# Centred x for the first two V and z2 blocks: an attention and gMLP kernel on one Trainium2 core

## The chip, the core and the metric

The kernel runs on one core of one Trainium2 chip. The core has TensorE (matrix products, written PE in the profile), VectorE (DVE), ScalarE (ACT), GpSimd (POOL), and SyncE (SP), which here only issues DMAs. Every engine works through its own instruction queue in order, and engines wait for one another by semaphores. Results of TensorE go to PSUM, which is used here as 8 banks of 128 x 512 fp32. Everything else lies in SBUF, 128 partitions wide. The metric is the device time of one execution in microseconds.

## The reference

For x of shape 2048 x 512 the reference adds a windowed attention and a gated MLP to x. Both start from the same normalised x.

```python
xn = layernorm(x)                                  # over 512, no gain or bias
qkv = xn @ wqkv                                    # 32 heads of 16; wqkv is 512 x 1536
logits[s, w] = q[s] . k[s - 2w] / 4                # w = 0..7; positions before 0 masked
o = softmax(logits over w) @ v[s - 2w]
a = o @ wo

z = gelu(xn @ w_in)                                # w_in is 512 x 1792
z1, z2 = z[:, :896], layernorm(z[:, 896:])
g = w_sp @ z2 + b_sp                               # w_sp is 2048 x 2048
out = x + a + (z1 * g) @ w_out                     # w_out is 896 x 512
```

V and z2 both have the form f(xn @ W). A row of xn is (x - mean) * rstd, so a row of xn @ W is rstd times a row of (x - mean) @ W. All matrices are bf16; sums are fp32.

## The kernel before

The 2048 rows of x are 16 blocks of 128 rows (b = 0 to 15), in four groups j of 512 rows. Nothing is written in program order by hand. The code adds tasks to a `Plan`, each with an engine, a function, an estimated duration, the buffers it reads and writes, and a priority (a low number goes first). `schedule` (line 121) then simulates the five engines with these estimates and puts the tasks of each engine in an order. At each step it takes, on the engine that can start earliest, the task with the lowest priority number among those ready within 40 ns of the first. It also picks the PSUM bank (`place`, line 148). `emit` (line 254) writes each engine's instructions in that order with the waits they need. On the chip the order is fixed: a task behind a late one waits too.

The stages around the change:

- **Loads** (lines 497 to 536). Block 0 of x is loaded in two halves of 64 partitions, one issued by SP and one by ACT (line 521). ACT then issues x1 and x2 (line 499). SP issues the halves of the V weights (wv, line 503), the halves of the z2 weights (w_in2, line 509), the other blocks of x, and the weights for Q and K (line 515).
- **Warm-up matmuls** (lines 538 to 543). 22 matmuls on zeros, 10 of 512 columns and 12 of 128, each with a bank of its own and priority 1000, so that the planner uses them where TensorE would otherwise idle.
- **Layer norm** (`ln_block`, line 551). Per block, VectorE computes statistics (L555), their aggregate (L557) and variance + eps (L559, called vpe). POOL raises that to the power -0.5, which is rstd (L561). VectorE then computes xn = (x - mean) * rstd (L563).
- **Transposes.** Blocks 0 to 3 of xn are transposed by TensorE against an identity (L573, four matmuls of 128 x 128) and copied from PSUM to the transposed tile xnT by ScalarE (L579), block 0 in two halves. Blocks 4 to 15 go through a transposing DMA issued by SP (L585).
- **V** (`v_block`, L598). Two tasks of two matmuls per block. ScalarE copies the result (L603) and POOL's queue writes it to a scratch tensor in DRAM (L606), from which shifted windows are read later.
- **z2** (`z2_block`, L696). Eight matmuls of 448 columns per block, then gelu with a row sum (L702) and a square with a row sum (L707) on ScalarE.
- **Q and K** (L615, copied by L624), which need all four blocks of their group. VectorE multiplies and adds the shifted products (L636, L641). z2 is normalised in waves of four blocks (L713 to L726), with POOL's pow at L723.
- **z1** (L740, L746), from the other half of w_in, the tile w_in1 (L771).
- **The tail.** The large product g = w_sp @ z2 (L823) with its copies and products (L831 to L837), the windowed sum over V (L851 to L857), its transposing DMA (L860), and the output products (L879, L888) with the final addition (L894) and store (L899).

The tiles share one arena. The place of w_in1 is used again for two small tiles late in the kernel (line 362).

Of the kernel before, what the change touches and what calls it, by code (L numbers as in the profile page):

```python
# [31 lines left out]
class Task:  # L32
    __slots__ = ("eng", "fn", "est", "name", "dma", "deps", "odeps", "idx", "start", "end", "eng_end", "count",
                 "tok", "clock", "prio", "tbl", "banks", "nwait", "ready", "outs", "used", "late")


class Plan:
# [37 lines left out]
    def add(self, eng, fn, reads=(), writes=(), est=100.0, name="", dma=None, prio=0.0, tbl=None, late=0.0, after=()):  # L75
        t = Task()
        t.eng, t.fn, t.est, t.name, t.dma, t.tbl = eng, fn, float(est), name, dma, tbl
# [43 lines left out]
    def schedule(self, dma_bw=300.0, xbar_bw=190.0, dma_lat=1300.0, dma_pre=400.0, issue=None, tol=40.0):  # L121
# [10 lines left out]
        free["sp"] = 810.0  # L132
# [15 lines left out]
        def place(b):  # L148
# [5 lines left out]
            for o in opts:  # L154
# [7 lines left out]
                key = (mate, av)  # L162
# [4 lines left out]
        while left:  # L167
            pick = None
            for e in ENGS:
                sc = []  # L170
                for t in cand[e]:
                    r = max(t.ready, free[e])
                    for b in t.banks:
                        if b.base is None:
                            p = place(b)
                            if p is None:
                                r = None
                                break
                            r = max(r, p[2])
# [14 lines left out]
            if pick is None:  # L194
                raise RuntimeError("scheduler stuck")
            r, e, t = pick
            for b in t.banks:
                if b.base is None:
                    _, o, av = place(b)
# [11 lines left out]
            if t.dma is not None:  # L211
                iss = issue[e]
# [117 lines left out]
def build_kernel(nc, A_x, A_wqkv, A_wo, B_x, B_w_in, B_w_sp, B_b_sp, B_w_out, out, report=False, emit=True):  # L330
# [12 lines left out]
    NWARM = 22  # L343
# [18 lines left out]
    place(3584, w_in1=0, tg=0, On=2048)  # L362
# [24 lines left out]
    with ExitStack() as es:  # L387
# [41 lines left out]
        for hf in range(2):  # L429
            R1(("xin0", hf), "xin", 256, 256 * hf)  # L430
        for s_ in range(1, NB):
# [25 lines left out]
        for hf in range(2):  # L457
            R(("xnT0", hf), "sb", [(off["xnT"] + dc * S, off["xnT"] + dc * S + 128) for dc in (2 * hf, 2 * hf + 1)])
# [38 lines left out]
        def ld_x(b, eng="sp"):  # L497
            sl = b
            return dma(eng, lambda e: e.dma_start(A("xin", 512, 512 * sl), x2[128 * b:128 * b + 128, :]), 128 * 512 * 2,
                ("xin", sl), writes=[("xin", sl)], name="ldx%d" % b)  # L500
# [19 lines left out]
        for hf, eng in ((0, "sp"), (1, "act")):  # L520
            dma(eng, (lambda hf: lambda e: e.dma_start(ar[64 * hf:64 * hf + 64, off["xin"]:off["xin"] + 512],
                                                       x2[64 * hf:64 * hf + 64, :]))(hf),
                64 * 512 * 2, ("xin0", hf), writes=[("xin0", hf)], name="ldx0_%d" % hf)
# [13 lines left out]

        for wi in range(NWARM):
            bw = plan.bank("warm%d" % wi)
# [427 lines left out]
```

## Time and profile before

| what | value |
|---|---|
| median of 3 runs | 241.43 us (241.14 to 241.65) |
| the profiled execution | 242.69 us |
| its span, first to last instruction | 239.3 us |
| granted TensorE clock, mean | 0.999 |
| busy: TensorE, VectorE, ScalarE, POOL | 234.0, 212.8, 98.1, 33.2 us |
| first V matmul | 7.28 us |
| DMA traffic | 42.81 MB, mean 179 GB/s |

Times in the profile count from the first instruction of the span. A row gives a group of instructions: line, engine, operation, what is written from what, and the shapes. "Idle before" is the time that the engine stood still just before them, and the name behind the arrow is what ended it. PEld is the loading of weights into TensorE, which overlaps with matmuls. Matmuls in a row overlap: one of 512 columns has a duration of 379 ns, but the starts of a row of them lie 216 ns apart. How fast they run is read from the distance of their starts. Some matmul records are missing from the trace (L823 has 440 matmuls to 448 weight loads), which looks like a hole of exactly one matmul.

### The profile page before, as it was taken

To read this page: it belongs to the slowest core of one execution; us is meant where nothing else is said; L and a number is where in the kernel's file an instruction comes from. 1 tells how busy PE (TensorE), PEld (TensorE's weight loads), DVE (VectorE), ACT (ScalarE), POOL (GpSimd) and SP (SyncE) were. 2 spreads that over 40 slices of the span, in tenths; PEclk is the share of its full clock that TensorE was granted. 3 is DMA by queue.
4 is the path that set the end of the run, shared out by engine and by line. 5 is a ranking of instruction groups with operands and counts; after the bars stand their busy time and mean duration, and the time that the engine had idled before them with its cause. 6 is when DMAs were issued, how large, how long until landed. Compare 5 with 4: busy or idle time off the path is not lost.

```text
span 239.3 us, 3165 instructions
## 1 busy us (share of the span) xinstructions
PE 234.0 (98%) x1212; PEld 112.7 (47%) x1233; DVE 212.8 (89%) x267; ACT 98.1 (41%) x144; POOL 33.2 (14%) x56
## 2 busy tenths in 40 slices
PE   7999999999999999999999999999999999999995
PEld 3555555555444444444454444444444444444444
DVE  3798889999989899999999999986898999999952
ACT  2596889899888975541112111001010100101100
POOL 2378350401383500000000000000000000000000
PEclk9999999999999999999999999999999999999999
DMA  5997969993327110004079999999999997942112
GB/s 185 364 316 145 224 151 215 208 208 76 114 108 244 62 37 10 0 8 170 0 228 320 182 245 258 267 168 294 309 344 244 282 325 244 271 141 55 22 44 66
DMA packets 77806, 42.81 MB, mean 179 GB/s; under 512 B 50129, under 2 KB 77153, under 8 KB 77793
## 3 DMA queue, kind: packets, MB, share of 16 engines
q1 hardware_dynamic: 76480, 40.13, 66.2%
q0 software_dynamic: 800, 2.11, 2.8%
q10 hardware_dynamic: 512, 0.38, 0.5%
q8 instruction: 9, 0.15, 0.2%
q14 instruction: 5, 0.03, 0.1%
HBM read 26.35 MB, written 4.21 MB: 128 GB/s over the span
## 4 chain that ended last, share of the span: by engine, by line
PE 69%; DVE 16%; POOL 7%; issue 4%; POOLq 1%; ACT 1%; DVEq 0%
PE ps L823 40%; PE ps L888 10%; PE ps L879 6%; DVE arena L641 5%; PE ps L598 5%; DVE arena L636 4%; PE ps L615 3%; POOL fpool L723 3%; DVE arena L726 2%; PE ps L696 2%; POOL fpool L561 2%; PE ps L541 2%; POOL vscr L606 1%; POOLq L387 1%; DVE arena L563 1%
## 5 line engine op out<-in xcount | busy, mean ns | idle before, releaser
L823 PE MATMUL ps<-arena 128*128 128x512 bf16 x440 | 98.6, 379 | 0.4
L823 PEld LDWEIGHTS ps<-arena 128*128 128x128 bf16 x448 | 43.7, 98 | 52.6
L831 ACT ACTIVATE arena<-ps 128x1024 bf16<-128x1024 f32 (+1 forms) x16 | 14.7, 917 | 104.4 <-PE ps L823 93.8
L636 DVE TENSOR_TENSOR arena<-arena 128x4096 bf16<-128x4096 bf16 x16 | 36.6, 2285 | 0.2
L851 DVE TENSOR_TENSOR arena<-arena 128x4096 bf16<-128x4096 bf16 x16 | 36.5, 2284 | 0.0
L854 DVE TENSOR_TENSOR arena<-arena 128x2048 bf16<-128x2048 bf16 (+1 forms) x32 | 30.5, 953 | 0.4
L615 PE MATMUL ps<-arena 128*128 128x512 bf16 x126 | 28.5, 379 | 0.1
L641 DVE TENSOR_TENSOR arena<-arena 128x4096 bf16<-128x4096 bf16 x12 | 27.5, 2288 | 0.2
L888 PE MATMUL ps<-arena 128*128 128x512 bf16 (+2 forms) x116 | 26.8, 366 | 0.2
L696 PE MATMUL ps<-arena 128*128 128x448 bf16 x128 | 26.0, 352 | 0.0
L740 PE MATMUL ps<-arena 128*128 128x512 bf16 x109 | 24.2, 379 | 0.2
L615 PEld LDWEIGHTS ps<-arena 128*128 128x128 bf16 x128 | 14.5, 113 | 13.0
L894 DVE TENSOR_TENSOR arena<-ps,arena 128x512 bf16<-128x512 f32 (+2 forms) x17 | 11.2, 657 | 9.4 <-PE ps L888 9.4
L624 ACT ACTIVATE arena<-ps 128x1024 bf16<-128x1024 f32 x16 | 16.2, 1019 | 4.3 <-PE ps L615 3.6
L696 PEld LDWEIGHTS ps<-arena 128*128 128x128 bf16 x128 | 12.4, 98 | 11.5
L888 PEld LDWEIGHTS ps<-arena 128*128 128x128 bf16 x119 | 11.6, 98 | 12.7
L740 PEld LDWEIGHTS ps<-arena 128*128 128x128 bf16 x112 | 10.8, 98 | 12.7
L746 ACT ACTIVATE arena<-ps 128x1024 bf16<-128x1024 f32 (+1 forms) x16 | 14.1, 916 | 6.1 <-PE ps L740 6.1
L879 PE MATMUL ps<-arena 128*128 128x512 bf16 (+2 forms) x67 | 16.5, 366 | 0.1
L702 ACT ACTIVATE arena<-ps 128x896 bf16<-128x896 f32 x16 | 14.6, 913 | 2.8 <-PE ps L696 2.6
L598 PE MATMUL ps<-arena 128*128 128x512 bf16 x60 | 14.9, 379 | 0.4 <-ACT arena L579 0.2
L707 ACT ACTIVATE arena<-arena 128x896 bf16<-128x896 bf16 x16 | 15.2, 949 | 0.2
(56 smaller groups left out, 176.4 us busy)
## 6 DMA issues: line engine op xcount, KB each, us to landing
arena<-vscr SPq DMA_DIRECT2D x16, 1024.0 KB, 6.8
arena<-in_A_x_dram SPq DMA_DIRECT2D x29, 128.0 KB, 5.3
vscr<-arena POOLq DMA_DIRECT2D x16, 128.0 KB, 2.8
out_dram<-arena SPq DMA_DIRECT2D x15, 128.0 KB, 5.1
arena<-in_A_wqkv_dram SPq DMA_DIRECT2D x2, 512.0 KB, 6.6
arena<-in_B_w_in_dram SPq DMA_DIRECT2D x2, 448.0 KB, 5.2
arena<-in_B_w_in_dram SPq DMA_DIRECT2D x1, 896.0 KB, 5.3
arena<-in_B_w_out_dram SPq DMA_DIRECT2D x1, 896.0 KB, 5.5
```

Source lines behind the costliest of these rows:

```text
L598: last = t.matmul(P(bk, 512), AC(off["xnT"] + dc * S + 128 * b, [[1, 128]]), AC(off["wv"] + 512 * dc, [[1, 512]]), start=(dc == 0), stop=( ...
L615: last = t.matmul(P(bk, 512, 512 * which), AC(off["wqk"] + 2048 * which + 512 * dc + c, [[4, 128]]), AC(off["xnT"] + dc * S + 512 * j, [[1 ...
L624: T("act", lambda a: a.activation(AC(qo, [[ko - qo, 2], [1, 512]]), P(bk, 1024).rearrange("p (t n) -> p t n", t=2), ACTF.Copy, scale=0.5), ...
L636: T("dve", (lambda pbv, qb, kb: lambda v: v.tensor_tensor(pbv, qb, kb, ALU.mult))(pbv, qb, kb), reads=rd, writes=[("pb", s_)], est=c_tt(40 ...
L641: T("dve", (lambda av, bv: lambda v: v.tensor_tensor(av, av, bv, ALU.add))(av, bv), reads=[("pb", 1)], writes=[("pb", acc)], est=c_tt(4096 ...
L696: last = t.matmul(P(bk, 448, 512 * hf), AC(off["xnT"] + dc * S + 128 * b, [[1, 128]]), AC(off["w_in2"] + 896 * dc + 448 * hf, [[1, 448]]), ...
L740: last = t.matmul(P(bk, 512, 512 * i), AC(off["w_in1"] + 896 * dc + 128 * fc, [[1, 128]]), AC(off["xnT"] + dc * S + 512 * j, [[1, 512]]), ...
L823: last = t.matmul(P(bk, 512, 512 * i), AC(off["z2"] + FH * sh + 128 * fc, [[1, 128]]), AC(off["wT%d" % r_] + sh * 512, [[1, 512]]), start= ...
L851: T("dve", lambda v: v.tensor_tensor(tv, tv, av, ALU.mult), reads=[("attn", b)], writes=[("Vs", sv)], est=c_tt(4096), name="pv%d" % b, pri ...
L854: T("dve", (lambda n: lambda v: v.tensor_tensor(A("Vs", n, 4096 * sv), A("Vs", n, 4096 * sv), A("Vs", n, 4096 * sv + n), ALU.add))(n), wri ...
L879: last = t.matmul(P(bk, cn), AC(off["OT"] + 512 * tb + 128 * cc, [[1, 128]]), AC(off["wo"] + 512 * cc + c0, [[1, cn]]), start=(cc == 0), s ...
L888: last = t.matmul(P(bk, cn), AC(off["z1T"] + fc * S + 128 * tb, [[1, 128]]), AC(off["w_out"] + 512 * fc + c0, [[1, cn]]), start=False, sto ...
```

## The change

For blocks 0 and 1 (`NCEN = 2`) VectorE now computes a centred tile xc = x - mean as soon as the mean is known. TensorE transposes xc, ScalarE copies it in two halves to a new tile xcT, and the V and z2 matmuls of these two blocks read xcT. The factor rstd is applied afterwards, as the per-partition `scale` of the ScalarE instruction that takes V or z2 out of PSUM. The normalised tile of blocks 0 and 1 is still made, transposed by TensorE and copied to xnT, since Q, K and z1 read it; these tasks have priorities behind the centred ones. Blocks 2 and 3 are as before.

Block 0 of x is loaded by one DMA from SP. x1 becomes the first load on ACT's queue. The warm-up is 24 matmuls, 8 of them long, all in one bank, and those left over are dropped once the planner's clock is past 9 us. xc and xcT lie in the place of w_in1, so that w_in1's load, whose code moves behind the V and z2 blocks, must wait for their readers.

The planner's own numbers change too: ordinary loads at 340 GB/s instead of 300, transposing DMAs at 300 instead of 190, 1.45 us of issue time for a transposing DMA instead of 0.48, and banks chosen by when they can be used, with 300 ns against a bank whose neighbour is free, instead of by the neighbour first.

```diff
@@ -118,7 +119,7 @@
...
-    def schedule(self, dma_bw=300.0, xbar_bw=190.0, dma_lat=1300.0, dma_pre=400.0, issue=None, tol=40.0):
+    def schedule(self, dma_bw=340.0, xbar_bw=300.0, dma_lat=1300.0, dma_pre=400.0, issue=None, tol=40.0):
...
@@ -129,7 +130,7 @@
...
         free["pool"] = 500.0
-        free["sp"] = 810.0
+        free["sp"] = 790.0
...
@@ -159,7 +160,7 @@
...
                     mate = 0.0 if (m["prev"] is not None and m["prev"].left > 0) else 1.0
-                key = (mate, av)
+                key = (max(av, now) + 300.0 * mate, av)
...
@@ -192,11 +193,30 @@
...
             r, e, t = pick
+            if t.drop and r > 9000.0:
+                t.start = t.end = t.eng_end = r
+                for b in t.banks:
+                    b.left -= 1
+                    if b.left == 0:
+                        for sl in slots:
+                            if sl["prev"] is b:
+                                sl["avail"] = r
+                cand[e].remove(t)
+                left -= 1
+                for o in t.outs:
+                    o.ready = max(o.ready, r)
+                    o.nwait -= 1
+                    if o.nwait == 0:
+                        cand[o.eng].append(o)
+                continue
...
                 if b.base is None:
-                    _, o, av = place(b)
+                    _, o, av = place(b, max(t.ready, free[e]))
...
@@ -209,7 +229,7 @@
...
             if t.dma is not None:
-                iss = issue[e]
+                iss = 1450.0 if t.dma.get("xbar") else issue[e]
...
@@ -340,7 +360,8 @@
...
     NXT = 4
-    NWARM = 22
+    NCEN = 2
+    NWARM = 24
...
@@ -359,7 +380,7 @@
...
     place(4 * S, xnT=0, OT=0)
-    place(3584, w_in1=0, tg=0, On=2048)
+    place(3584, w_in1=0, tg=0, On=2048, xcT=0, xc=2048)
...
@@ -517,10 +539,7 @@
...
-        for hf, eng in ((0, "sp"), (1, "act")):
-            dma(eng, (lambda hf: lambda e: e.dma_start(ar[64 * hf:64 * hf + 64, off["xin"]:off["xin"] + 512],
-                                                       x2[64 * hf:64 * hf + 64, :]))(hf),
-                64 * 512 * 2, ("xin0", hf), writes=[("xin0", hf)], name="ldx0_%d" % hf)
+        ld_x(0, "sp")
...
@@ -535,12 +554,12 @@
...
+        bw = plan.bank("warm")
         for wi in range(NWARM):
-            bw = plan.bank("warm%d" % wi)
-            n_ = 512 if wi < NWARM - 12 else 128
+            n_ = 512 if wi < 8 else 128
...
                                                        stop=True))(bw, n_),
-              reads=["zeros"], writes=[bw], est=(427.0 if n_ == 512 else 75.0), name="warm%d" % wi, prio=1000)
+              reads=["zeros"], writes=[bw], est=(427.0 if n_ == 512 else 107.0), name="warm%d" % wi, prio=1000, drop=True)
...
@@ -551,41 +570,64 @@
...
             xs_ = b
+            xk = [("xin", xs_)]
             xin = A("xin", 512, 512 * xs_)
-            T("dve", lambda v: v.bn_stats(Fv("st6", 6, 6 * b), xin), reads=([("xin", xs_)] if b else [("xin0", 0), ("xin0", 1)]), writes=[("st6", b)],
+            T("dve", lambda v: v.bn_stats(Fv("st6", 6, 6 * b), xin), reads=xk, writes=[("st6", b)],
...
               writes=[("mv", b)], est=178, name="bnag%d" % b, prio=-1 + b * 0.1)
-            T("dve", lambda v: v.tensor_scalar(Fv("vpe", 1, b), Fv("mv", 1, 2 * b + 1), LN_EPS, None, ALU.add),
-              reads=[("mv", b)], writes=[("vpe", b)], est=140, name="vpe%d" % b, prio=-1.5 + b * 0.1)
-            lnr.append(T("pool", lambda g: g.tensor_tensor(Fv("rstd", 1, b), Fv("vpe", 1, b), Fv("mhalf", 1), ALU.pow),
-                         reads=[("vpe", b), "mhalf"], writes=[("rstd", b)], est=550, name="rstd%d" % b, prio=0))
-            T("dve", lambda v: v.tensor_scalar(A("xn", 512, 512 * sl), xin, Fv("mv", 1, 2 * b),
-                                               Fv("rstd", 1, b), ALU.subtract, ALU.mult),
-              reads=([("xin", xs_)] if b else [("xin0", 0), ("xin0", 1)]) + [("mv", b), ("rstd", b)], writes=[("xn", sl)], est=c_ts(512),
-              name="norm%d" % b, prio=-1 + b * 0.1)
-            if b < NXT:
-                bk = plan.bank("xTr%d" % b)
+            early = b < NCEN
+            xn = A("xn", 512, 512 * sl)
+
+            def pe_tr(src, key, name, prio):
+                bk = plan.bank(name)
...
                     for dc in range(4):
-                        last = t.matmul(P(bk, 128, 128 * dc), A("xn", 128, 512 * sl + 128 * dc), ident, start=True,
+                        last = t.matmul(P(bk, 128, 128 * dc), src[:, 128 * dc:128 * dc + 128], ident, start=True,
...
                     return last
-                T("pe", tr, reads=[("xn", sl), "ident"], writes=[bk], est=4 * c_mm(128), name="xTr%d" % b, prio=0)
-                for hf in ((0, 1) if b == 0 else (None,)):
-                    d0, dn = (0, 4) if hf is None else (2 * hf, 2)
-                    T("act", (lambda d0, dn: lambda a: a.activation(
-                        AC(off["xnT"] + d0 * S + 128 * b, [[S, dn], [1, 128]]),
-                        P(bk, 128 * dn, 128 * d0).rearrange("p (c n) -> p c n", c=dn), ACTF.Copy))(d0, dn),
-                      reads=[bk], writes=([("xnT", b)] if hf is None else [("xnT0", hf)]), est=c_act(128 * dn),
-                      name="xTe%d_%d" % (b, d0), prio=0)
-            else:
-                return dma("sp", lambda e: e.dma_start_transpose(AC(off["xnT"] + 128 * b, [[S, 4], [1, 128]]),
-                                                          A("xn", 512, 512 * sl)),
-                    128 * 512 * 2, ("xT", sl), reads=[("xn", sl)], writes=[("xnT", b)], name="xTd%d" % b,
-                    xbar=True, prio=1)
+                T("pe", tr, reads=[key, "ident"], writes=[bk], est=4 * c_mm(128), name=name, prio=prio)
+                return bk
+
+            if early:
+                xc = A("xc", 512, 512 * b)
+                T("dve", lambda v: v.tensor_scalar(xc, xin, Fv("mv", 1, 2 * b), None, ALU.subtract),
+                  reads=xk + [("mv", b)], writes=[("xc", b)], est=360, name="cen%d" % b, prio=-1 + b * 0.1)
+                bk = pe_tr(xc, ("xc", b), "xTc%d" % b, 0)
+                for hf in range(2):
+                    T("act", (lambda hf: lambda a: a.activation(
+                        A("xcT", 256, 512 * b + 256 * hf), P(bk, 256, 256 * hf), ACTF.Copy))(hf),
+                      reads=[bk], writes=[("xcT", b, hf)], est=c_act(256), name="xTe%d_%d" % (b, hf), prio=0)
+            T("dve", lambda v: v.tensor_scalar(Fv("vpe", 1, b), Fv("mv", 1, 2 * b + 1), LN_EPS, None, ALU.add),
+              reads=[("mv", b)], writes=[("vpe", b)], est=140, name="vpe%d" % b,
+              prio=(-0.5 if early else -1.5) + b * 0.1)
+            lnr.append(T("pool", lambda g: g.tensor_tensor(Fv("rstd", 1, b), Fv("vpe", 1, b), Fv("mhalf", 1), ALU.pow),
+                         reads=[("vpe", b), "mhalf"], writes=[("rstd", b)], est=550, name="rstd%d" % b, prio=0))
+            T("dve", lambda v: v.tensor_scalar(xn, xin, Fv("mv", 1, 2 * b), Fv("rstd", 1, b), ALU.subtract, ALU.mult),
+              reads=xk + [("mv", b), ("rstd", b)], writes=[("xn", sl)], est=c_ts(512),
+              name="norm%d" % b, prio=(0.35 + b * 0.01 if early else -1 + b * 0.1))
+            if b < NXT:
+                bk2 = pe_tr(xn, ("xn", sl), "xTr%d" % b, 0.5)
+                T("act", lambda a: a.activation(AC(off["xnT"] + 128 * b, [[S, 4], [1, 128]]),
+                                                P(bk2, 512).rearrange("p (c n) -> p c n", c=4), ACTF.Copy),
+                  reads=[bk2], writes=[("xnT", b)], est=c_act(512), name="xTn%d" % b, prio=0.5)
+                return None
+            return dma("sp", lambda e: e.dma_start_transpose(AC(off["xnT"] + 128 * b, [[S, 4], [1, 128]]), xn),
+                       128 * 512 * 2, ("xT", sl), reads=[("xn", sl)], writes=[("xnT", b)], name="xTd%d" % b,
+                       xbar=True, prio=1)
+
+        def xTv(b, dc):
+            if b < NCEN:
+                return A("xcT", 128, 512 * b + 128 * dc)
+            return AC(off["xnT"] + dc * S + 128 * b, [[1, 128]])
+
+        def xsc(b):
+            return Fv("rstd", 1, b) if b < NCEN else 1.0
+
+        def xrk(b):
+            return [("rstd", b)] if b < NCEN else []
...
@@ -595,13 +637,13 @@
...
                     for dc in (2 * hf, 2 * hf + 1):
-                        last = t.matmul(P(bk, 512), AC(off["xnT"] + dc * S + 128 * b, [[1, 128]]),
+                        last = t.matmul(P(bk, 512), xTv(b, dc),
...
                     return last
-                T("pe", mm, reads=[("xnT", b) if b else ("xnT0", hf), ("wv", hf)], writes=[bk], est=2 * c_mm(512), name="V%d_%d" % (b, hf),
+                T("pe", mm, reads=[("xcT", b, hf) if b < NCEN else ("xnT", b), ("wv", hf)], writes=[bk], est=2 * c_mm(512), name="V%d_%d" % (b, hf),
...
             T("act", lambda a: a.activation(A("Vn", 512, 512 * sl).rearrange("p (d h) -> p d h", d=16),
-                                            PC(bk.col(), [[1, 16], [16, 32]]), ACTF.Copy), reads=[bk],
+                                            PC(bk.col(), [[1, 16], [16, 32]]), ACTF.Copy, scale=xsc(b)), reads=[bk] + xrk(b),
...
@@ -693,16 +735,16 @@
...
                     for dc in range(4):
-                        last = t.matmul(P(bk, 448, 512 * hf), AC(off["xnT"] + dc * S + 128 * b, [[1, 128]]),
+                        last = t.matmul(P(bk, 448, 512 * hf), xTv(b, dc),
...
                     return last
-                T("pe", mm, reads=[("xnT", b), ("w_in2a", "w_in2b")[hf]], writes=[bk], est=4 * c_mm(448),
+                T("pe", mm, reads=([("xcT", b, 0), ("xcT", b, 1)] if b < NCEN else [("xnT", b)]) + [("w_in2a", "w_in2b")[hf]], writes=[bk], est=4 * c_mm(448),
...
                                             PC(bk.col(), [[512, 2], [1, 448]]),
-                                            ACTF.Gelu_apprx_tanh, accum_out=Fv("s1", 1, b)),
-              reads=[bk], writes=[("z2", b), ("s1", b)], est=c_act(FH, accum=True),
+                                            ACTF.Gelu_apprx_tanh, scale=xsc(b), accum_out=Fv("s1", 1, b)),
+              reads=[bk] + xrk(b), writes=[("z2", b), ("s1", b)], est=c_act(FH, accum=True),
...
@@ -768,13 +810,13 @@
...
-        dma("sp", lambda e: e.dma_start(A("w_in1", 3584).rearrange("p (c n) -> p c n", c=4),
-                                        B_w_in[:, 0:896].rearrange("(c p) n -> p c n", p=128)),
-            512 * 896 * 2, "w_in1", writes=["w_in1"], name="ldwin1", prio=2, after=lnd[4:8])
...
             z2_block(b)
+        dma("sp", lambda e: e.dma_start(A("w_in1", 3584).rearrange("p (c n) -> p c n", c=4),
+                                        B_w_in[:, 0:896].rearrange("(c p) n -> p c n", p=128)),
+            512 * 896 * 2, "w_in1", writes=["w_in1"], name="ldwin1", prio=2, after=lnd[4:8])
```

## The prediction

> **What bounds the kernel now.** I read the page's busy table first, then the stretches (busy time of each engine by stage), then the chain that ended last at both ends, then the opening in order of time.
>
> The page's first table, with the busy time and share of the span:
> ```profile
> span 239.3 us, 3165 instructions
> PE 234.0 (98%) x1212; PEld 112.7 (47%) x1233; DVE 212.8 (89%) x267; ACT 98.1 (41%) x144; POOL 33.2 (14%) x56
> ```
> The stretches; columns after the length are busy time of PE, weight loads, DVE, ACT and POOL with instruction counts:
> ```profile
> 0.00:7.28 7.28, 5.81 (x23) 2.74 (x24) 3.33 (x10) 1.93 (x4) 1.87 (x9) 1.00 0.67 215
> 7.28:14.66 7.38, 7.33 (x43) 3.75 (x45) 5.67 (x20) 5.61 (x11) 3.46 (x6) 1.00 1.09 361
> 14.66:21.57 6.91, 6.91 (x33) 3.61 (x32) 5.99 (x20) 5.39 (x8) 5.49 (x18) 1.00 0.92 190
> 21.57:53.00 31.43, 31.32 (x183) 16.77 (x185) 28.58 (x47) 27.12 (x47) 9.71 (x10) 1.00 1.01 202
> ```
> From 7.28 us, the first V matmul, TensorE idles 0.05, 0.00 and 0.11 us per stretch. So the end is the start of that matmul, plus TensorE's work in a row, plus a tail of 2.8 us (236.5 to 239.3). A gain can come from an earlier start or less TensorE work; an added wait is paid in full. What sets 7.28 is in the opening (start, duration, engine, line, operation, and in brackets the idle time before and its releaser):
> ```profile
> 1.25 5.09 PE L541 MATMUL ps<-arena 128*128 128x512 bf16 x16 [1.25 <-DVE arena L494]
> 3.32 0.69 DVE L555 BATCH_NORM_STATS2 fpool<-arena 128x6 f32<-128x512 bf16 x1 [2.13 <-DMA arena<-in_A_x_dram]
> 4.05 0.18 DVE L557 BATCH_NORM_AGGREGATE fpool<-fpool 128x2 f32<-128x6 f32 x1
> 4.27 0.15 DVE L559 TENSOR_SCALAR fpool<-fpool 128x1 f32<-128x1 f32 x1
> 4.51 0.56 POOL L561 TENSOR_TENSOR fpool<-fpool 128x1 f32<-128x1 f32 x1 [2.93 <-DVE fpool L559]
> 5.13 0.69 DVE L555 BATCH_NORM_STATS2 fpool<-arena 128x6 f32<-128x512 bf16 x1 [0.71 <-DMA arena<-in_A_x_dram]
> 5.75 0.40 DVE L563 TENSOR_SCALAR arena<-arena,fpool 128x512 bf16<-128x512 bf16 x1
> 6.20 0.61 PE L573 MATMUL ps<-arena 128*128 128x128 bf16 x4
> 6.60 0.47 PE L541 MATMUL ps<-arena 128*128 128x128 bf16 x3
> 6.84 0.66 ACT L579 ACTIVATE arena<-ps 128x256 bf16<-128x256 f32 x2 [2.55 <-PE ps L573]
> 7.28 1.04 PE L598 MATMUL ps<-arena 128*128 128x512 bf16 x4 [0.22 <-ACT arena L579]
> 8.15 0.39 PE L573 MATMUL ps<-arena 128*128 128x128 bf16 x4
> ```
> rstd of block 0 is ready at 5.07, but its normalisation runs at 5.75: on VectorE it stands behind block 1's statistics, which wait 0.71 us for x1. The chain of waits over this window is warm-up matmuls, L573, L579, L598. The L541 matmuls start 0.43 us apart for 512 columns; the V matmuls start 0.216 apart ((1.04 - 0.39) / 3). The four transposes take 0.61 us at 6.20 and 0.39 at 8.15. So TensorE runs at half rate up to 6.81 (last start of the three L541) and at full rate by 7.28; the trace's clock record opens at 6.87.
>
> **The change, part by part.** The profiled execution took 242.69 us: its span of 239.3 and 3.4 around it. It stands 1.26 over the median of 241.43. I sum against its span and carry the difference to the median.
>
> *Start of V.* Out of block 0's chain go vpe (0.15), POOL's pow (0.56) with its hops, and the wait behind block 1; in comes a subtraction of 128x512 bf16 (L563's row, 0.40). If x0 lands as before, statistics start at 3.32, the aggregate ends at 4.23, the centring at about 4.67, and TensorE could transpose at 4.72. It is not free: warm-ups stand ahead of it in its in-order queue. Worked from the planner's estimates (read for the order alone: x0 at 3.57, statistics 0.685, aggregate 0.178, centring 0.36), the plan has the transposes ready at 4.90, after 8 long and 4 short warm-ups. On the chip those take 1.25 + 8 x 0.43 + 4 x 0.107 = 5.08 (the first start gap is a little shorter). From the first transpose to the first V took 7.28 - 6.20 = 1.08, which stays: V at about 6.18. Gain 1.09. Bounds: two warm-ups fewer or four more give 5.95 to 6.6, so 1.3 to 0.7.
>
> *x0 whole on SP, x1 first on ACT's queue.* The halves took 0.59 and 0.57 to issue and 2.1 and 2.4 to land. x1's issue moves from 1.42 to about 0.81; beside wv0 on SP it took 0.85 to issue and landed at 5.11, 3.7 later. x0 on one queue lands between 3.0 (as a half) and 4.5 (like x1). Nearest is the half, issued first on an idle queue: 3.0 to 3.6, all hidden under the warm-ups, which cover up to 3.6. Beyond that each us costs one. ACT's queue loses an issue; SP's second issue may slip 0.3, but wv0 (landed 4.73) has 1.4 to spare.
>
> *Half-rate V.* V now starts inside the slow time. From 6.18 to 6.87 is 0.69 us at half rate: 0.34 lost. Bounds 0 (full rate from 6.18) to 0.55 (slow until 7.28).
>
> *Extra transposes.* Blocks 0 and 1 are transposed twice: 8 more matmuls at (0.39 - 0.22) / 3 = 0.056, so +0.44, all on TensorE and all paid.
>
> *Warm-ups behind V0.* 24 instead of 22, 8 of them long. By the same working some three fall among V0, block 1's transposes and V1. 3 x 0.056 = +0.17; bounds 0 to 0.4 (six, some at half rate).
>
> *V1's wait.* Block 1's transposes are queued after V0's first pair, at about 7.04 in slow time; 0.44 to the copy and 0.44 to the matmul (as 6.84 and 7.28 show) against V0's second pair: +0.14; bounds 0 to 0.5. The gap of 0.14 ahead of V at 9.49, where V1 and V2 follow a transpose, goes: -0.14 (bounds 0 to -0.22 with the one at 11.3).
>
> *VectorE and POOL.* Two centrings, +0.8 us of VectorE, lie in its waits before 10 us (0.71 for x1, 0.66 and 0.66 for POOL). Without that cover block 2's normalisation (8.46) slips by as much, and TensorE has z2 of blocks 0 and 1 meanwhile. POOL keeps its two pows; the copies of V0 and z2 of block 0 now wait for rstd, done at 5.07, before them by over 2 us. The normalised blocks 0 and 1 come later, first needed by Q and K at 14.66.
>
> *ScalarE.* Block 1's copy (0.59) becomes two (0.66 together as for block 0), and two whole copies come in (0.59 each): +1.25 us. Idle in 7.28 to 14.66: 7.38 - 5.61 = 1.77, which hides it, and 1.09 more from the earlier start. Four evictions take their scale from a tensor instead of a constant; no row shows that, between 0 and 0.2 us each, off the path, taken as 0. [...]
>
> *w_in1's load* now must wait for the matmuls that read the centred tiles lying in its place (z2 of block 1, about 14 us); it was issued at 20.37 and L740 first reads it at 75.7: nothing.
>
> *The planner.* A transpose DMA is now booked at 1.45 us of issue instead of 0.48 (rows: 28 transposes of activations at 1.2 to 1.6, of w_sp at 2.2), loads are booked faster, banks are chosen by earliest start. The whole order can move. With TensorE idle almost nowhere there is nothing to win; 0 to +1 us, taken as 0, since no wait after 10 us is for a DMA and the last transposed block lands 1.8 us before its matmul (232.35 against 234.13).
>
> Sum: -1.09 + 0.34 + 0.44 + 0.17 + 0.14 - 0.14 = **-0.14 us**: span 239.16, execution 242.55, median **241.3**.
>
> **The rivals.**
> *A, clock early and a clean order.* If full rate comes before 6.18 (-0.34) and neither warm-ups nor a copy stand in V1's way (-0.31), the gain is 0.79: 240.65. For it: nothing ties 6.87 to V. Against: warm-ups begin at 1.25 as before and one profile shows one moment. [...]
>
> *B, ScalarE becomes the bound (slower).* From 21.57 to 53 it is busy 27.12 of 31.43. If the 1.25 us of added copies are not absorbed by 14.66, evictions run late, PSUM banks come free late and TensorE waits for a bank in the Q, K and z2 stage. It decides once more than about 0.6 us is left over; at most 1.25: 241.9 to 242.55. For it: 86% busy there. Against: ScalarE's waits on PE, 0.3 to 0.7 us before Q, K and z2 copies, are slack.
>
> *C, x0 late.* Landing at 3.9 to 4.3 puts V at 6.5 to 6.9: 241.6 to 242.0.
>
> *D, the new order stalls TensorE later.* Some 0.5 to 1 us: 241.8 to 242.3.
>
> **How the numbers follow.** Forecast 0.40, A 0.20, B 0.18, C 0.10, D 0.12. What a measurement here can tell from no change is about 0.2%, 0.48 us: faster is under 240.95, slower over 241.91. Faster: A whole and 0.10 of the forecast, from the fast-clock end alone: 0.30. Slower: 0.16 of B, 0.04 of C, 0.09 of D: 0.29. Within: 0.41. The range 240.6 to 242.3 leaves out 0.07 of A, 0.08 of B and 0.03 of D.
>
> **What would show it.** Right: the first centred transposes at about 5.1, directly behind a warm-up; V at 6.2, its first matmuls 0.43 apart; TensorE idle under 0.3 us from V to 14; L823 starting as densely as before. Wrong: V0 behind a DMA wait of VectorE; TensorE gaps between 14 and 53 with PSUM copies late; full rate seen before 6.2; or TensorE waiting for a transfer after 100 us.

## The result and the profile after

The median after is 250.34 us (249.41 to 251.24, 6 runs) against 241.45 us before in the same comparison (6 runs): a ratio of 1.0359, 95% interval 1.032 to 1.0398. The kernel became 3.6% slower. The prediction said 241.3 us in a range of 240.6 to 242.3, so it is wrong by 9 us. The profiled execution took 251.24 us with a span of 248.4.

Line numbers moved: L588 is a transpose by TensorE, L640 V, L738 z2, L865 the product g, L838 the transposing load of w_sp, L902 the transposing DMA of an attention block, L921 the output product that reads that block, L930 the other output product.

From the page of the changed kernel: the busy table, the granted TensorE clock in 40 equal slices of 6.2 us, and the costliest row of idle time:
```profile
span 248.4 us, 3215 instructions
PE 238.1 (96%) x1240; PEld 113.5 (46%) x1240; DVE 214.5 (86%) x269; ACT 98.9 (40%) x147; POOL 33.0 (13%) x56
...
PEclk9999999999999999999999995899999999999999
...
L921 PE MATMUL ps<-arena 128*128 128x512 bf16 (+2 forms) x68 | 17.5, 381 | 6.2 <-DMA arena<-arena 6.2
```
TensorE was busy 98% before and is now 96% of a longer span. One row holds 6.2 us of idle time, ended by a DMA from arena to arena: that is L902. In slices 25 and 26, 149 to 161 us, the clock is below full. Neither was there before.

The stretches, with the columns that the prediction showed:
```profile
0.00:7.28 7.28, 6.03 (x31) 3.30 (x32) 3.86 (x13) 2.23 (x5) 1.95 (x10) 1.00 0.69 224
7.28:14.66 7.38, 7.37 (x51) 3.91 (x50) 5.30 (x16) 6.31 (x13) 3.16 (x6) 1.00 1.09 365
...
21.57:53.00 31.43, 31.43 (x186) 16.74 (x185) 28.25 (x46) 27.09 (x48) 11.75 (x13) 1.00 0.97 197
...
101.20:236.50 135.30, 129.06 (x612) 57.90 (x611) 120.43 (x126) 17.07 (x19) 0.00 (x0) 0.97 0.76 194
```
The last of these stretches in the kernel before:
```profile
101.20:236.50 135.30, 134.67 (x655) 62.62 (x666) 123.19 (x133) 18.67 (x20) 0.00 (x0) 1.00 0.76 197
```
Up to 53 us TensorE is as dense as before. The loss is in the last stretch: 6.24 us of idle time against 0.63, and a mean clock of 0.97. The first matmul of g starts at 100.52 us against 101.02 before, so the changed kernel was half a microsecond ahead there and ended 9.1 us behind (spans 248.4 and 239.3).

The place, on TensorE in order of time:
```profile
138.66 6.85 PE L865 MATMUL ps<-arena 128*128 128x512 bf16 x31
150.78 1.89 PE L921 MATMUL ps<-arena 128*128 128x512 bf16 x4 [5.26 <-DMA arena<-arena]
152.46 3.19 PE L930 MATMUL ps<-arena 128*128 128x512 bf16 x7
155.44 4.16 PE L865 MATMUL ps<-arena 128*128 128x512 bf16 x16
```
The first output product is due at 145.35 us, one matmul after the last of g, and starts at 150.78; the profile counts 5.26 us of that as idle. The matmuls behind it start 0.427 us apart (7 of L930 take 3.19) instead of 0.216: the trace's clock record says half rate from 149.705 for 6.827 us. In the kernel before, the same product (L879) starts without a wait:
```profile
137.65 10.95 PE L823 MATMUL ps<-arena 128*128 128x512 bf16 x49
148.44 1.03 PE L879 MATMUL ps<-arena 128*128 128x512 bf16 x4
```

What it waits for is on SP's queue. First before, then after (start, time that SP's queue was held, line, count):
```profile
124.50 17.40 SPq L796 DMA_TRANSPOSE arena<-in_B_w_sp_dram  x5
141.95 1.27 SPq L860 DMA_TRANSPOSE arena<-arena  x1
```
```profile
124.81 22.52 SPq L838 DMA_TRANSPOSE arena<-in_B_w_sp_dram  x7
147.38 1.27 SPq L902 DMA_TRANSPOSE arena<-arena  x1
```
Attention block 0 is transposed by a DMA that SP issues. Five w_sp transposes stood ahead of it before, seven stand there now, and it is issued 5.4 us later. Its data was there in time: VectorE had ended block 0's sum at 138.5 before and at 138.2 after, so in the changed kernel the transfer stood 9.2 us on SP's queue with its data ready. At the same time TensorE asks for it earlier, after 204 matmuls of g instead of 216. These are the moments of the first four blocks, read from the trace (landing is the last completion event of the transfer, use the first matmul of L921 or L879):

| kernel | issued | landed | used |
|---|---|---|---|
| before | 141.9, 148.6, 158.0, 161.1 | 144.6, 151.3, 160.6, 167.1 | 148.4, 155.1, 164.4, 170.2 |
| after | 147.4, 154.2, 156.2, 162.0 | 150.7, 156.8, 161.7, 167.3 | 150.8, 159.4, 162.7, 167.4 |

Before, each block lands 3 to 4 us ahead of its use. After, blocks 0 and 3 are used at the moment they land. The two are late for different reasons: block 0 stood on SP's queue, block 3 was issued 0.03 us after VectorE ended its sum (161.97). VectorE itself had been held up, since a later block's sum needs an output buffer that block 0's transfer still reads:
```profile
144.55 1.95 DVE L896 TENSOR_TENSOR arena<-arena 128x2048 bf16<-128x2048 bf16 x2
150.75 0.42 DVE L899 TENSOR_TENSOR arena<-arena 128x512 bf16<-128x512 bf16 x1 [4.25 <-DMA arena<-arena]
```
The account from 100.52 us on: 6.2 us of waits (5.26 and two of 0.44 and 0.54 at 167.4 and 217.3), some 0.17 more at each of the three restarts (the profile counts idle time from a modelled end of the matmul before), and about 2.8 from the half rate (the 14 matmuls between 150.78 and 156.63 take 5.85 us where 14 x 0.216 = 3.02) make 9.5 of the 9.6 us lost.

The front did what the change says. TensorE at the opening:
```profile
1.25 4.02 PE L560 MATMUL ps<-arena 128*128 128x512 bf16 x12 [1.25 <-DVE arena L516]
5.06 0.63 PE L588 MATMUL ps<-arena 128*128 128x128 bf16 x4
5.49 0.85 PE L560 MATMUL ps<-arena 128*128 128x128 bf16 x6
6.26 0.61 PE L640 MATMUL ps<-arena 128*128 128x512 bf16 x2
...
6.99 0.59 PE L640 MATMUL ps<-arena 128*128 128x512 bf16 x2
```
The centred transposes start at 5.06, V at 6.26 instead of 7.28.

### The profile page after: what moved, and what is told of

It reads as the page before. It is cut to its first block, busy times and chain, and to the rows that moved or that the text cites. A ratio compares the mean times of both kernels' runs of the same rounds, so it can differ in the third digit from the quotient of the medians.

```text
span 248.4 us, 3215 instructions
## 1 busy us (share of the span) xinstructions
PE 238.1 (96%) x1240; PEld 113.5 (46%) x1240; DVE 214.5 (86%) x269; ACT 98.9 (40%) x147; POOL 33.0 (13%) x56
## 4 chain that ended last, share of the span: by engine, by line
PE 63%; DVE 12%; SPq 9%; POOL 8%; DMA 6%; issue 2%; ACT 1%; DVEq 0%
PE ps L865 27%; PE ps L782 10%; SPq L838 9%; PE ps L930 8%; DMA arena<-arena 6%; PE ps L921 5%; PE ps L640 5%; POOL fpool L606 4%; PE ps L657 3%; POOL fpool L765 2%; PE ps L560 2%; PE ps L738 2%; DVE arena L678 2%; DVE arena L683 2%; DVE arena L608 1%
## 5 line engine op out<-in xcount | busy, mean ns | idle before, releaser
L865 PE MATMUL ps<-arena 128*128 128x512 bf16 x448 | 99.5, 380 | 0.0
L865 PEld LDWEIGHTS ps<-arena 128*128 128x128 bf16 x448 | 43.9, 98 | 53.1 <-issue 1.3
L657 PE MATMUL ps<-arena 128*128 128x512 bf16 x128 | 28.8, 379 | 0.0
L930 PE MATMUL ps<-arena 128*128 128x512 bf16 (+2 forms) x119 | 28.6, 381 | 0.0
L738 PE MATMUL ps<-arena 128*128 128x448 bf16 x128 | 26.0, 352 | 0.2 <-DVE arena L706 0.2
L782 PE MATMUL ps<-arena 128*128 128x512 bf16 x112 | 24.5, 379 | 0.0
L921 PE MATMUL ps<-arena 128*128 128x512 bf16 (+2 forms) x68 | 17.5, 381 | 6.2 <-DMA arena<-arena 6.2
L930 PEld LDWEIGHTS ps<-arena 128*128 128x128 bf16 x119 | 11.9, 101 | 13.8 <-issue 1.9
L738 PEld LDWEIGHTS ps<-arena 128*128 128x128 bf16 x128 | 12.3, 98 | 12.0 <-DVE arena L706 0.7
L640 PE MATMUL ps<-arena 128*128 128x512 bf16 x64 | 15.6, 379 | 0.0
L876 DVE TENSOR_TENSOR arena<-arena 128x1024 bf16<-128x1024 bf16 (+1 forms) x16 | 9.9, 619 | 5.2 <-ACT arena L873 5.2
```

The costliest lines, as they stand in the source:

```text
L640: last = t.matmul(P(bk, 512), xTv(b, dc), AC(off["wv"] + 512 * dc, [[1, 512]]), start=(dc == 0), stop=(dc == 3))
L657: last = t.matmul(P(bk, 512, 512 * which), AC(off["wqk"] + 2048 * which + 512 * dc + c, [[4, 128]]), AC(off["xnT"] + dc * S + 512 * j, [[1 ...
L738: last = t.matmul(P(bk, 448, 512 * hf), xTv(b, dc), AC(off["w_in2"] + 896 * dc + 448 * hf, [[1, 448]]), start=(dc == 0), stop=(dc == 3))
L782: last = t.matmul(P(bk, 512, 512 * i), AC(off["w_in1"] + 896 * dc + 128 * fc, [[1, 128]]), AC(off["xnT"] + dc * S + 512 * j, [[1, 512]]), ...
L865: last = t.matmul(P(bk, 512, 512 * i), AC(off["z2"] + FH * sh + 128 * fc, [[1, 128]]), AC(off["wT%d" % r_] + sh * 512, [[1, 512]]), start= ...
L921: last = t.matmul(P(bk, cn), AC(off["OT"] + 512 * tb + 128 * cc, [[1, 128]]), AC(off["wo"] + 512 * cc + c0, [[1, cn]]), start=(cc == 0), s ...
```

## The experiments

The theory: the loss comes from the planner's figures alone, not from the centred tiles. The plan books transfers one after another. At 300 GB/s instead of 190, the transfer of one w_sp transpose (128 x 2048 bf16, 524 KB) is booked at 524/300 = 1.75 us, beside 1.45 us of SP's queue; seven in a row are booked at 12.2 us of transfer and held SP's queue for 22.5. So the plan puts more of them ahead of attention block 0 and lets TensorE ask for the attention blocks early. The rival: the centred front or its new loads disturb the later stages. Within the theory a second question was which part costs: the place on SP's queue, TensorE's early asking, or the half rate after the wait.

### e1: the changed kernel with the old planning figures

```diff
-    def schedule(self, dma_bw=340.0, xbar_bw=300.0, ...
+    def schedule(self, dma_bw=300.0, xbar_bw=190.0, ...
...
-                iss = 1450.0 if t.dma.get("xbar") else issue[e]
+                iss = issue[e]
```
Expected:

> The changed kernel with the planner's three DMA figures put back (300 and 190 GB/s, 0.48 us of issue for every DMA), all else as changed. Theory Q (the loss is the order on SP's queue: the transposing DMA of attention block 0 stands behind seven w_sp transposes, and TensorE's first attention product waits for it): five w_sp transposes stand ahead of it again as in the kernel before, its issue comes at about 142, it lands at about 145.5, and TensorE asks for it at 100.7 + 220 x 0.216 + 0.8 = 149: no wait, no half-rate stretch. The front then shows alone: V at 6.26, g starting 0.5 earlier (100.67 against 101.19), so 240.9 us, between 240.6 and 241.3. Rival F (the centring, the bank choice or the added copies cost the time): still above 247.

Measured: 240.65 us (240.18 to 241.29, 10 runs), ratio 0.9958 (0.9938 to 0.9977). The page of this kernel, and its first output product:
```profile
span 238.8 us, 3214 instructions
PE 234.9 (98%) x1240; PEld 113.3 (47%) x1240; DVE 213.6 (89%) x269; ACT 98.9 (41%) x147; POOL 31.2 (13%) x56
```
```profile
148.79 1.03 PE L921 MATMUL ps<-arena 128*128 128x512 bf16 x4
```
Block 0 lands at 145.2 and is used at 148.8. After V starts, no wait of TensorE is over 0.2 us. Three numbers put back remove the whole loss, and the kernel is then faster than both: 0.4% below before.

### e2: the kernel before with the new planning figures

```diff
-    def schedule(self, dma_bw=300.0, xbar_bw=190.0, ...
+    def schedule(self, dma_bw=340.0, xbar_bw=300.0, ...
...
-                iss = issue[e]
+                iss = 1450.0 if t.dma.get("xbar") else issue[e]
```
Expected:

> The kernel before with only the planner's three DMA figures of the change (340 and 300 GB/s, 1.45 us of issue for a transposing DMA). Theory Q: seven w_sp transposes at 2.2 to 2.7 us stand ahead of attention block 0's transposing DMA, TensorE asks for it after 200 g matmuls, at 101.2 + 43.1 + 0.8 = 145.1, and gets it at 150.7: a wait of 5 to 6 us, a half-rate stretch after it costing about 2.9, in all 249.5 to 251. Rival F: 241.4, as before.

Measured: 252.91 us (250.95 to 254.36, 4 runs), ratio 1.0452 (1.0401 to 1.0503). TensorE around the place:
```profile
139.80 7.07 PE L823 MATMUL ps<-arena 128*128 128x512 bf16 x32
151.97 1.86 PE L879 MATMUL ps<-arena 128*128 128x512 bf16 x4 [5.10 <-DMA arena<-arena]
153.63 3.19 PE L888 MATMUL ps<-arena 128*128 128x512 bf16 x7
```
The same wait and the same half rate (6.83 us of it) in a kernel without a centred tile. With e1 this settles the first question: the figures are the cause, and the centred front is not. The median is some 2 us over what was expected; in the profile a wait for VectorE, 1.06 us in the distance of the starts at 98.9, and two of 0.39 and 0.49 between 73 and 76 come on top, which the changed kernel does not have.

### e3: the changed kernel with only the transposes booked at 190 GB/s

```diff
-    def schedule(self, dma_bw=340.0, xbar_bw=300.0, ...
+    def schedule(self, dma_bw=340.0, xbar_bw=190.0, ...
```
Expected:

> The changed kernel with one figure put back: transposing DMAs booked at 190 GB/s instead of 300; 340 GB/s for loads and 1.45 us of issue stay. Theory Q with the booked bandwidth as its cause: six w_sp transposes stand ahead, 124.8 + 6 x 2.6 + the first one's slow start of about 4 put the attention block's issue at 144.5 and its landing at 148; TensorE asks after 224 g matmuls, at 149.8: no wait, 240.9 us (240.6 to 241.5). Rival I (the issue figure of 1.45 us is the cause): still 249 to 251.

Measured: 241.78 us (241.08 to 242.61, 12 runs), ratio 1.0001 (0.9982 to 1.0021). Block 0 lands at 147.1 and is used at 150.0. Of the three figures this one carries the loss. The median is 0.3 us over the expected range, and the last 0.4% to e1 is not cleared up: the two spans differ by only 0.3 us (239.1 and 238.8), the profile shows one wait more, 0.53 us at 53.3, and one block lands 0.2 us before its use. No run separates the load figure from the issue time.

### e4: zero matmuls in the place of the wait

22 matmuls of 512 columns on zeros, ahead of the first output product, keep TensorE busy through most of the 5.26 us. The later matmuls overwrite what they write.
```diff
+                    if tb == 0:
+                        def fill(t):
+                            ...
+                            for _ in range(22):
+                                last = t.matmul(P(bk, cn), zeros[:, 0:128], zeros[:, 0:cn], start=True, stop=True)
...
```
Expected:

> The changed kernel with 22 matmuls on zeros of 512 columns put on TensorE's queue directly ahead of the first attention product, into the bank that this product then overwrites; the planner counts them as nothing, so every order stays. They need 22 x 0.216 = 4.75 us and fit into the wait of 5.4. Theory H (the half-rate stretch of 6.8 us behind the wait is the answer to TensorE standing idle): the wait of TensorE for the DMA stays, the stretch goes, and 5.75 us of it at half rate give back 2.9: 247.4 us. Rival (the stretch has another cause, or the stall is made up elsewhere): unchanged at 250.3, or slower by up to 4.75.

Measured: 250.43 us (249.14 to 250.53, 4 runs), ratio 1.0343 (1.0309 to 1.0376): no gain over the changed kernel, where 3 us were expected. The output products of the first three blocks:
```profile
150.71 1.02 PE L921 MATMUL ps<-arena 128*128 128x512 bf16 x4 [0.53 <-DMA arena<-arena]
157.77 1.02 PE L921 MATMUL ps<-arena 128*128 128x512 bf16 x4 [1.08 <-DMA arena<-arena]
162.25 1.02 PE L921 MATMUL ps<-arena 128*128 128x512 bf16 x4 [1.08 <-DMA arena<-arena]
```
The clock is full throughout (granted clock 1.0), so the half rate did come from the idle time. But blocks 1 and 2, which the slow matmuls gave time to land, are now waited for. The 2.8 us of half rate in the account above are therefore mostly not a price of their own: without them the transfers, not the clock, set the pace.

### e5: four w_sp transposes moved back on SP's queue only

```diff
+        sp = plan.order["sp"]
+        for p_ in range(4):
+            t = [t for t in sp if t.name == "wT3_%d" % p_][0]
+            sp.remove(t)
+            sp.insert([t.name for t in sp].index("OTd%d" % (3 + p_)) + 1, t)
```
Expected:

> The changed kernel with all its figures; only on SP's queue the four w_sp transposes of the last row group are moved behind the transposing DMAs of attention blocks 3, 4, 5 and 6. The orders of the other engines stay. Theory Q (a place on a queue): four w_sp transposes remain ahead, which ended at 139.9 in the changed kernel; the DMA of block 0 is then issued at 139.9, lands by 143.2, and TensorE asks at 145.35: no wait, no half-rate stretch, 240.4 to 241.7 us (up to 1 of small waits, since TensorE's order asks for blocks 1 to 3 early). Rival (VectorE or the transfer bandwidth is late, and the queue only shows it): 246 to 250.

Measured: 247.88 us (247.71 to 249.01, 5 runs), ratio 1.028 (1.0244 to 1.0316). The time lies outside what the theory expected and in the range of its rival, that VectorE or the transfers are late. Block 0 now lands at 142.7 and is used at 145.5 without a wait, and the clock stays full (1.0). But blocks 4, 5 and 7 are waited for:
```profile
167.20 1.02 PE L921 MATMUL ps<-arena 128*128 128x512 bf16 x4 [1.68 <-DMA arena<-arena]
174.22 1.04 PE L921 MATMUL ps<-arena 128*128 128x512 bf16 x4 [1.90 <-DMA arena<-arena]
...
188.59 1.04 PE L921 MATMUL ps<-arena 128*128 128x512 bf16 x4 [1.48 <-DMA arena<-arena]
```
SP's queue held up only block 5 of these by much (sum ended at 166.1, issued at 168.4); blocks 4 and 7 were issued 0.03 and 0.17 us after VectorE ended their sums, and then took 6.0 and 6.1 us to land. Landings of 5.7 to 6.8 us stand at blocks 3 to 7 of e1 too, without a wait. Blocks 4 and 5 land earlier here than in e1 (167.1 and 174.2 against 172.2 and 176.5), and are waited for all the same, since TensorE asks for them earlier still; block 7 lands 2.5 us later than in e1. So the reading "block 0 stands too far back on SP's queue" is not the whole of it, and I changed the theory: TensorE's early asking is the larger part. e9 and e10 test that.

### e9 and e10: SP's order exchanged between e1 and the changed kernel

e9 is e1 with SP's order of the changed kernel, e10 the changed kernel with SP's order of e1. All other engines keep theirs.
```diff
+        rank = {n: i for i, n in enumerate((
+            "ldx0 ldwv0 ldwv1 ldwin20 ldx3 ...
+        plan.order["sp"].sort(key=lambda t: rank[t.name])
```
Expected:

> The kernel of e1 with only SP's queue in the changed kernel's order (seven w_sp transposes ahead of attention block 0's), all other engines as in e1. If TensorE's early asking is the larger part of the loss: block 0 lands near 150.7, is asked near 148.8, TensorE waits about 1.9 us with no half-rate stretch behind it, VectorE stands about 4 us for its output buffer, and later slack takes most of it: 242.5 to 244. If the place on SP's queue is the whole of it: 247 to 251, as the changed kernel.

> The changed kernel with only SP's queue in e1's order (five w_sp transposes ahead of attention block 0's), all other engines as in the changed kernel. If TensorE's early asking is the larger part: block 0 lands near 145.2 against an ask at 145.35, no wait there, but blocks 1 to 3 land near 154.7, 161.2 and 167.5 as in e1 against asks near 151, 154.5 and 159, waits of 2 to 3.6 us each: 247 to 249. If the place on SP's queue is the whole of it: 240.5 to 242, no wait of TensorE over 0.3 us.

Measured: e9 242.32 us (241.94 to 243.17, 10 runs), ratio 1.0033 (1.0019 to 1.0048); e10 251.13 us (250.73 to 251.67, 4 runs), ratio 1.0392 (1.0365 to 1.0419). TensorE in e9, then in e10:
```profile
149.53 1.04 PE L921 MATMUL ps<-arena 128*128 128x512 bf16 x4 [1.11 <-DMA arena<-arena]
...
201.64 1.04 PE L921 MATMUL ps<-arena 128*128 128x512 bf16 x4 [0.35 <-DMA arena<-arena]
208.20 1.04 PE L921 MATMUL ps<-arena 128*128 128x512 bf16 x4 [0.56 <-DMA arena<-arena]
```
```profile
145.90 1.03 PE L921 MATMUL ps<-arena 128*128 128x512 bf16 x4
...
154.28 1.02 PE L921 MATMUL ps<-arena 128*128 128x512 bf16 x4 [2.39 <-DMA arena<-arena]
...
160.66 1.87 PE L921 MATMUL ps<-arena 128*128 128x512 bf16 x4 [2.99 <-DMA arena<-arena]
...
168.02 0.82 PE L921 MATMUL ps<-arena 128*128 128x512 bf16 x3 [1.46 <-DMA arena<-arena]
```
SP's new order alone costs 1.7 us (242.32 against 240.65), 0.2 us less than expected, and VectorE's expected stand for an output buffer did not come. SP's old order alone saves nothing. In e10 blocks 0 to 3 land at 145.4, 154.1, 160.5 and 168.0, within 0.7 us of e1's 145.2, 154.7, 161.2 and 167.5, and e1 uses them at 148.8, 158.1, 164.8 and 170.6. With landings as good as equal, it is the earlier asking on TensorE that makes the 6.8 us of waits for blocks 1 to 3, and a half-rate stretch of 3.41 us behind the one of 2.99. That stretch was not expected; its 8 matmuls at 0.211 us extra are 1.7 of the 2.1 us by which e10 is over its range. Some 0.8 us of e10's distance to e1 lies earlier (g starts at 101.29 against 100.51). VectorE keeps the changed kernel's order in e10 too; since blocks 0 to 3 land no later, and their sums end 3.9 to 10.5 us ahead of their issues, that order is not what makes TensorE wait there. No run exchanges TensorE's order alone.

### e6, e7, e8: what the front is worth

All three start from e1. e6 sets `NCEN = 0`: no centred tile, every block as before, with the new loads and warm-ups. e7 loads block 0 in two halves again, with x1 second on ACT's queue. e8 makes the eight second transposes of blocks 0 and 1 six times over, 40 matmuls more.
```diff
# e6
-    NCEN = 2
+    NCEN = 0
# e7
-        ld_x(0, "sp")
+        for hf, eng in ((0, "sp"), (1, "act")):
+            dma(eng, ...
...
# e8
-                    for dc in range(4):
+                    for dc in list(range(4)) * (6 if early and name.startswith("xTr") else 1):
```
Expected:

> The kernel of e1_front without centring (NCEN 0): x0 whole on SP, x1 first on ACT, 24 warm-ups, the new bank rule. Theory C (the centring moves V, the loads alone little): 8 long and 12 short warm-ups stand ahead of the first transposes, 1.25 + 3.39 + 1.28 = 5.92, V 1.08 to 1.2 later at 7.0 to 7.2 against 7.28; no extra transposes: 241.2 us (241.0 to 241.5). Rival L (x1's early landing, 3.65 instead of 5.11, is what gains): 240.65 or less.

> The kernel of e1_front with x0 in two halves and x1 second on ACT's queue, as before the change. x0 is as early, so V stays at 6.2 to 6.3. x1 lands at about 5.1, its centred tile is ready at 6.4 instead of 6.05, and six warm-ups and a transpose stand between block 1's transposes and V1: V1 at 8.1 to 8.4 instead of 8.07. If x1 early matters: 0.2 to 0.5 slower than e1_front, 240.9 to 241.2. If not: 240.65.

> The kernel of e1_front with each of the eight second transposes (normalised blocks 0 and 1) done six times instead of once, into the same place: 40 more matmuls of 128 columns, 40 x 0.056 = 2.2 us of TensorE that no order counts on. Theory P (TensorE is the bound from the first V to the end, so that every such us is paid): 240.65 + 2.2 = 242.9 us. Rival (slack later takes it up): 240.7 to 241.5.

Measured:

| run | median us | ratio to before (95%) | V starts | last Q/K matmul |
|---|---|---|---|---|
| e1 | 240.65 (10 runs) | 0.9958 (0.9938 to 0.9977) | 6.26 | 64.58 |
| e6, no centring | 241.04 (12 runs) | 0.9982 (0.9964 to 1.0) | 6.87 | 63.86 |
| e7, x0 in halves | 241.94 (11 runs) | 1.0023 (1.0004 to 1.0042) | 6.26 | 64.70 |
| e8, 40 more | 242.68 (11 runs) | 1.0046 (1.0027 to 1.0064) | 5.93 | 65.86 |

e8: 40 matmuls at 0.0555 us are 2.2 us, and 2.03 were paid. TensorE is the bound there, as the prediction's base claim says. e7 came out some 0.7 us over its expectation: V1 waits 0.50 us for its copy, and two waits of 0.28 and 0.36 appear at 99.7 and 123.2. The wait of V1 fits the loading (x1 lands at 5.18 instead of 3.61); the later two need not come from it, since e6 and e7 are planned anew and the later orders move too (216 matmuls of g stand ahead of attention block 0 in e7, 220 in e1). e6 fits its expectation: the centring is worth 0.4 us in the medians, with intervals that overlap. The last column shows that this isn't won in the front: without centring the last Q/K matmul comes 0.7 us earlier, with 8 transposes less and the full clock already there when V starts (5.04 us, against 7.22 in e1). In this profile e6 loses 0.45 us of that later, in waits of 0.16 and 0.29 us at 73.8 and 98.1, and still ends first (spans 238.5 and 238.8). So that the centring gains anything is not shown.

## Why the prediction was wrong, point by point

- *The planner* is the step that failed: "0 to +1 us, taken as 0, since no wait after 10 us is for a DMA and the last transposed block lands 1.8 us before its matmul". It measured about +9 us. What came in its place is TensorE asking for the attention blocks ahead of their landing, in an order that the new booked rate made. Three things were wrong in the step. A wait that is absent in the old order says nothing about an order made with other numbers. Nor does a slack in the old order: the prediction looked at the last block, and block 0, whose slack before was 3.8 us, is the one that came to be waited for 5.26 us. And of the new figures only the issue time was held against rows, and there too the w_sp transposes (2.2 by the prediction, 17.4/5 = 3.5 in the row of five) stood above the 1.45 booked. The rate was not held against anything: five w_sp transposes held SP's queue for 17.4 us before, against 5 x 1.75 = 8.7 of transfer booked by the new figure and 5 x 2.76 = 13.8 by the old one.
- Rival *D* named the right kind of event and gave it 0.5 to 1 us. The size failed: one wait alone is 5.26 us, since the order on TensorE and the order on SP's queue moved against each other. Of the two, TensorE's is the larger part (e9 and e10). The sign listed last under "wrong", TensorE waiting for a transfer after 100 us, is the one that came.
- The base claim holds: an added wait or matmul is paid nearly in full (e8: 2.03 of 2.2; account above: 9.5 of 9.6). Its limit is e4: where two causes stand in a row, taking away one gives nothing.
- *Start of V*: 6.26 against 6.18 predicted, a gain of 1.02 against 1.09; the transposes at 5.06 against 5.08. Right.
- *x0 whole on SP, x1 first on ACT's queue*: x0 lands at 3.46 (3.0 to 3.6 predicted), x1 at 3.65 instead of 5.11. Hidden, right, and rival *C* is out.
- *Half-rate V*: 0.34 with bounds 0 and 0.55. The full clock comes at 6.35 in this profile, which costs about 0.04; in e1 at 7.22, about 0.48. Both bounds were needed.
- *Extra transposes* and *Warm-ups behind V0*: 8 transposes and 3 warm-ups, as predicted. *V1's wait*: 0.10 against 0.14. The gap at 9.30 is gone, but one of 0.18 came at 11.26, so the -0.14 was not won.
- *ScalarE*: 6.31 us busy between 7.28 and 14.66, and no wait of TensorE followed. Rival *B* is out. The rows that the trace of before could not show are there now, of V (L645) and z2 (L744):
```profile
L744 ACT ACTIVATE arena<-ps 128x896 bf16<-128x896 f32 x14 | 12.7, 911 | 2.1 <-PE ps L738 2.0
...
L645 ACT ACTIVATE arena<-ps 128x512 bf16<-128x512 f32 x14 | 7.9, 599 | 0.5 <-PE ps L640 0.5
...
L744 ACT ACTIVATE arena<-ps,fpool 128x896 bf16<-128x896 f32 x2 | 2.0, 1007 | 0.8 <-PE ps L738 0.8
L645 ACT ACTIVATE arena<-ps,fpool 128x512 bf16<-128x512 f32 x2 | 1.4, 689 | 0.3 <-PE ps L640 0.3
```
  With the scale from a tensor (fpool) one of V takes 689 ns instead of 599, one of z2 1007 instead of 911: 90 and 96 ns more.
- The sum of the front, -0.14, can be read at the last Q/K matmul, the same work in both orders: 64.49 before, 64.52 after, a difference of +0.03, with a wait of 0.36 us at 53.1 in it that the sum did not have. In e1 it is +0.09, in e9 -0.44 (full clock at 5.72). So the front was sized within 0.3 us, and is worth close to nothing.
- Rival *A*, 240.65, is by accident e1's median, for another reason: of e1's gain over before, 0.59 us in the profiles are two gaps ahead of the 128x32 matmuls of L649 (0.31 at 74.4, 0.28 at 98.9) that e1's profile does not have. Which part of the change closes them, no run tells.

Left open: what e3 lacks to e1, and what TensorE's new order would cost alone, with every other queue as in e1.

## What to carry to other kernels

When a change touches the numbers of a planner, it changes every order in the kernel: list each transfer that an engine waits for late in the run, with its landing and its use, and hold every booked rate against what the queue took in the trace (1.75 us booked, 3.2 us held). A late transfer has two sides, its place on the issuing queue and the moment its reader asks; exchanging one engine's order at a time, as in e9 and e10, tells which. And a front that starts a microsecond earlier can be worth nothing if it pays for it in extra work on the engine that is the bound.

## What the runs showed of the hardware

- w_sp transposes hold SP's queue for unequal times: in the changed kernel the first of the seven took 7.60 us, the other six 2.0 to 2.7, and one behind an attention transpose 4.62. What the first waits for, no view tells. The mean over the seven is 22.52/7 = 3.2 us, 163 GB/s, while DMA moved 241 GB/s in that stretch.
- The trace's clock record of the changed kernel has full rate from 6.345 and half rate from 149.705, 143.360 us later; the half-rate stretch lasts 6.827 us and the full rate behind it 92.160. In the kernel before, the full rate that opens at 6.87 lasts 232.106 us. In e10 the half rate lasts 3.41, half of 6.827; 3.4133 goes into the four lengths 42, 2, 27 and 68 times. Full rate first came at 6.87 in the kernel before, 6.35 in the changed one, 7.22 in e1, 5.04 in e6 and 5.72 in e9.
- Idle times of TensorE up to 1.90 us did not lower the clock in e4, e5 and e9 (granted clock 1.0 in each). In e10 the clock stayed full through the wait of 2.39 us; behind the one of 2.99 the matmuls ran at half rate (four in 1.87 us instead of 1.02), for 3.41 us. In the changed kernel the clock fell 1.07 us before the end of the wait of 5.26, for 6.83 us, and in e2 1.4 us before the end of the one of 5.10, also for 6.83. What decides whether a wait lowers the clock, and for how long, no run here tells.
